# A residual block of attention and a gated MLP: score tiles moved from the attention stage to the projection stage, and one PSUM copy moved to VectorE

## The chip, the cores and the metric

The kernel runs on one core of one Trainium2 chip. The metric is device time in microseconds; of the kernel before, three runs gave 1596.11, 1596.20 and 1596.48 us, the median is 1596.2 us. A core has a matrix engine (TensorE, PE in the profile; its weight loads are listed apart as PEld), a vector engine (VectorE, DVE), a scalar engine (ScalarE, ACT), a general engine (GpSimd, POOL) and a queue engine that starts transfers (SyncE, SP). TensorE writes to PSUM, which here is used as eight tiles ("banks") of 128 x 512 float32.

## What is computed

The input is x, 2048 tokens of 512 features. With 32 heads of 16 features:

```
xn = layernorm(x)
q, k, v = split(xn @ wqkv)                      # 32 heads of 16
p = softmax(q @ k.T / 4)                        # per head, 2048 x 2048
s = (p @ v) @ wo
g = silu(gelu(xn @ w1 + b1) @ w2 + b2)          # 1376 hidden features
out = x + s * g
```

For the softmax the kernel subtracts from every score the maximum of its query's row. The scores are therefore computed twice: once with queries on the partitions, only to find the row maxima, and once transposed, with keys on the partitions, where the (negated) maximum is added through two more contraction rows and the exponential is taken. This document calls the first kind **score tiles** and the second kind **transposed tiles**.

## The kernel before, in words

The work is cut into 32 **units** u: eight groups g of four heads, times four chunks c of 512 queries (`g, c = divmod(u, 4)`). A unit has 64 score tiles (128 queries x 512 keys of one head; two heads run on the two halves, "sides", of TensorE's rows at the same time) and 64 transposed tiles (16 blocks of 128 keys x 4 heads). All 2048 score tiles are made in the order of the list `heads`, unit after unit, well ahead of the transposed tiles of the same unit, because the maxima have to be transposed (`s_end1`, line 265), copied, written to DRAM and loaded back (`load_mh`, line 148) first.

**First stage (projections).** Layer norm, v, q, k and the two MLP products run as float32r pieces of 64 rows, two at a time on the two sides of TensorE (`run` and `mm`, lines 584 to 622; all at L591). Between them `fill` (line 564) puts score tiles, the "early" ones. `LEAD` is their number in units of four: 144, so 576 tiles, nine units. `ROWS` (line 562) is the number of matmuls that one side has left, so a side gets its next early tile once its count `row[a]` has reached `FILL0 + put + made * ROWS / (4 * LEAD)`. A score tile is one matmul (L183) into one of two banks, `ps_a` or `ps_b` (the ring `s_ring`, handed out in turn by `s_tile`, line 92), and one VectorE reduction with max over 512 columns (L189), after which the bank is free again.

**Second stage (attention).** It is a hand-written order of steps n = 0 to 512 (lines 967 to 985). Step n makes the four transposed tiles of unit n // 16 and key block n % 16 (letter T: one matmul at L740, one exponential on ScalarE at L742) and adds the block of the step before to the unit's sum p @ v (letter V: `pv_step`, eight matmuls at L805 into the one bank `ps_v`). The transposed tiles rotate through four banks. The rest of the score tiles is spread over the steps by `due(n)`: two in step 1, three in each of the steps 2 to 491, none later. The strings in `ORDER` (line 40) say how: with three tiles `TXSTTSTYV`, where S is a whole score tile and X and Y are the halves of a third one, one for each side, joined in one bank; with none `TTTTV`. Y waits for a token that passes through GpSimd's queue (lines 221 and 228). The ring of the score tiles has three banks here (`ps_x` joins at line 774).

When a unit's 16th block has been added (V of step 16u + 16), its 128 x 512 sums are copied from PSUM to SBUF by ScalarE (L812), so that `ps_v` is free for the next unit; the last unit's copy is shared by ScalarE and VectorE (L814, L815). One step later SyncE's queue moves the copied rows on (`o_move`), later the denominators are inverted (`o_den`) and multiplied in by GpSimd (`o_div`).

Keys: the buffers `kts` hold three groups (KB = 3). Group 3 takes the place of group 0, whose last reader is unit 3's transposed tiles (steps 48 to 63; step 48 + b reads key block b). Its keys are loaded by six transfers of GpSimd's queue in steps 56 to 61 (first half of the keys) and six in steps 64 to 69. Unit 12, the first of group 3, makes its score tiles in the order of the key chunks of 512 (`at_of`, line 172).

**Tail.** From step 492 on, when no score tiles are left, finished tokens are projected by `wo` (`w_token`, `w_mul`) and gated.

Of the kernel before, what the change touches and what calls it, by code (L numbers as in the profile page):

```python
# [10 lines left out]
AF = mybir.ActivationFunctionType  # L11
# [6 lines left out]
S = 2048  # L18
# [5 lines left out]
CH = 512  # L24
NCH = S // CH
# [4 lines left out]
EPS = 1e-5  # L30
SCALE = DH ** -0.5
VW = DH + 1
LEAD = 144
NW = 10
EARLY = 4
DONE = 492
FILL0 = 30
HB = 4
W2B = 2
ORDER = {0: "TTTTV", 3: "TXSTTSTYV"}  # L40
HC = CH // 2
PAIRED = 28
KB = 3
# [5 lines left out]
def fused(ctx: ExitStack, tc: tile.TileContext, x, wqk, wv, wo, w1, b1, w2, b2, out):  # L49
    nc = tc.nc  # L50
# [37 lines left out]
    NU = NG * NCH  # L88
# [40 lines left out]
    def q_rows(qs, u, sides=range(2)):  # L129
        g, c = divmod(u, NCH)  # L130
        for a in sides:
            for b, src in enumerate((qk_h, qk_l, qk_h)):
                r = 64 * a + DH * b
                nc.sync.dma_start(qs[r:r + DH].bitcast(F32), rows(src, g, 0, a, c * CH, CH))

    def load_qs(u, sides=range(2)):
        if u < NU:
            QS[u] = qzs[u % 2] if u < LEAD // 16 else qss[0][:, u % 2]
            q_rows(QS[u], u, sides)
# [18 lines left out]
    def units_of(u):  # L158
        return (u,) if u >= PAIRED else (u - u % 2, u - u % 2 + 1)

    def tick():
        for e in later:
            e[0] -= 1

    def flush():
        while later and later[0][0] <= 0:
            u = later.pop(0)[1]
            run_off()
            s_end1(u)
            s_end2(u)  # L170
# [38 lines left out]
    def s_op(op):  # L209
        if op == "S":  # L210
            if whole:
                s_whole(whole.pop(), 1)
            else:
                whole.append(jobs.pop(0))
                s_whole(whole[0], 0)
        elif op == "X":
            if not cut:
                cut[:] = [jobs.pop(0), 0]
            ps, pool = s_tile(True)
            x = s_mm(ps, cut[0], 0, 0, cut[1] * HC, HC)  # L220
            token = nc.gpsimd.nop().ins
            tc.add_manual_dep(token, x.name, SYNC, reason="row tile done")
            cut[2:] = [ps, pool, token]
            run_off()
        else:
            job, n, ps, pool, token = cut
            y = s_mm(ps, job, 1, HC, n * HC, HC)
            tc.add_manual_dep(y, token.name, SYNC, reason="other row tile")
            s_max(ps, job, slice(0, 2), n)
            s_ring.append(pool)  # L230
            cut[1] += 1
            if n:
                cut.clear()
# [72 lines left out]
    for i in range(nu):  # L306
        pairs.append(ms[2 * i:2 * i + 2])
        if (i + 1) * len(qs) // nu > i * len(qs) // nu:
            g, c = qs[i * len(qs) // nu]
# [4 lines left out]
    for j in range(len(pairs)):  # L314
        for h in range(2):
# [4 lines left out]
            due = next((i for i in range(j, len(pairs)) if is_m[i]), len(pairs))  # L320
            nxt = next((i for i in range(j + h, len(pairs)) if is_m[i]), len(pairs))
            left = 2 * (nxt - j) + 1 - h
            need = 4 * sum(is_m[:nxt]) - 4 - nd
            room = 2 * (due + 1 - j) - h
            n = 2 if nd < len(parts) and parts[nd][2] and ready - nd > room else 1
            n = max(n, need - 2 * (left - 1))
# [234 lines left out]
    ndown = sum(1 for e in plan if e[0] == "down")  # L561
    ROWS = 12 * (4 * VQ + 2 * len(pairs)) + 6 * ndown - 10 + 2 * LEAD - 2 * (LEAD // 32) - FILL0

    def fill(a):
        due = FILL0 + put[0] + sum(made) * ROWS // (4 * LEAD)
        if sum(made) < 4 * LEAD and row[a] >= due and (made[0] <= made[1]) == (a == 0):
            taken()
            if later and later[0][0] <= 0:
                put[0] += 2
                u = later.pop(0)[1]  # L570
                s_end1(u)
                s_end2(u)
                return
            s_one(a)
            row[a] += 1
            tick()

    def taken():
        prog["pe"] += 1
        s_when.append(prog["pe"])  # L580
        if len(s_when) > 2:
            prog["seen"] = max(prog["seen"], s_when[-3])
# [150 lines left out]
    def t_one(u, k, p, a):  # L733
        g = u // NCH
        if (u, k) not in PT:
            PT[u, k] = slot(3 + len(PN) % 3, (P, GH, CH))
            PN.append(1)
        ps = t_tile()
        r = slice(64 * a, 64 * a + 3 * DH + 2)
        nc.tensor.matmul(ps, kts[g % KB][p][r, k * P:(k + 1) * P],  # L740
                         QT[u][r, p, :], start=True, stop=True)
        nc.scalar.activation(PT[u, k][:, 2 * p + a, :], ps, AF.Exp, scale=SCALE)  # L742
# [55 lines left out]
    PV, OS, DN, DR = {}, {}, {}, {}  # L798
    def pv_step(u, k):
        g = u // NCH  # L800
        if k == 0:
            PV[u] = ps_v.tile([P, CH], F32, name="pv")
        for j in range(GH):
            h = (g * GH + j) * VW
            nc.tensor.matmul(PV[u][32 * j:32 * j + 32, :], vsb[:, k, h:h + 32], PT[u, k][:, j, :],  # L805
                             start=(k == 0), stop=(k == NT - 1))
        del PT[u, k]
        if k == NT - 1:
            OS[u] = wb.tile([P, CH], F32, name="os", bufs=1)
            pv = PV.pop(u)  # L810
            if u < NU - 1:
                nc.scalar.activation(OS[u], pv, AF.Copy)  # L812
            else:
                nc.scalar.activation(OS[u][:, :HC], pv[:, :HC], AF.Copy)  # L814
                nc.vector.tensor_copy(OS[u][:, HC:], pv[:, HC:])  # L815
# [104 lines left out]
    def at(n, f, *a, pos=3):  # L920
        todo.setdefault((n, pos), []).append((f, a))

    KS = tuple(range(KT))
    L = 16 * NU

    def due(n):
        return min(4 * L, 4 * LEAD + max(0, 3 * n - 1))

    for u in range(NU):
        g, c = divmod(u, NCH)  # L930
        if c == 0 and g == KB:
            for i in range(6):
                at(56 + i, load_k, g, (i,), nc.gpsimd, 0, S // 2)
                at(64 + i, load_k, g, (i,), nc.gpsimd, S // 2, S // 2)
        elif c == 0 and g > KB:
            for i in range(6):
                at(64 * (g - KB + 1) + 6 + i, load_k, g, (i,), nc.gpsimd)
        if u >= 2:
            at(16 * u - 14, load_qt, u)
            need = min(n for n in range(L) if due(n) >= 64 * (units_of(u)[-1] + 1)) + (4 if u < NU - 1 else 2)  # L940
            at(max(16 * u - 14, need), load_mh, u)
        if u < NU - 1:
            at(16 * u + 17, o_move, u, pos=0)
            at(16 * u + (25 if u < NU - 2 else 19), o_den, u, pos=0)
            at(16 * u + (31 if u < NU - 2 else 22), o_div, u, nc.gpsimd)
    T3 = range(NT - NCH, NT)
    late = range(NW, NT)
    for t in range(NW):
        n = DONE + 2 * t
# [6 lines left out]
    for i, t in enumerate(late):  # L956
        n = L - 2 * len(late) - 1 + 2 * i
# [8 lines left out]
    jobs.extend(heads[made[0]:])  # L966
    for n in range(L + 1):
        ua, ka = divmod(n, 16)
        want = due(n) - due(n - 1)
        i = 0  # L970
        for op in ORDER[want] if n > 1 else ("TTTTV", "TTSTSVT")[n]:
            if op in "SXY":
                s_op(op)
            elif op == "V":
                if n:
                    pv_step(*divmod(n - 1, 16))
                for _ in range(4):
                    tick()
                flush()
            else:  # L980
                if EARLY <= 4 * n + i < 4 * L:
                    t_one(ua, ka, i % 2, 1 - i // 2)
                for f, args in todo.get((n, i), []):
                    f(*args)
                i += 1
# [54 lines left out]
```

## Time and profile before

| | |
|---|---|
| median of three runs | 1596.2 us |
| span of the profiled execution, first to last instruction | 1594.7 us |
| median less span | 1.5 us |
| granted TensorE clock | 1.000 |
| busy, share of the span: PE / PEld / DVE / ACT / POOL | 100% / 57% / 87% / 79% / 23% |
| score reductions L189 | 2048, mean 685 ns |
| exponentials L742 | 2048, mean 612 and 613 ns |
| first stage with early score tiles | about 59 to 476 us |
| steps with score tiles | about 476 to 1507 us |

The profiled execution's own time is its span; the median of the runs lies 1.5 us above it. Durations are those of single instructions; consecutive instructions of an engine overlap at their ends, so that 2048 exponentials of 612 ns fill less than 2048 times 612 ns, and an engine's busy time counts such an overlap once. The starts of PE's matmuls are recorded, their ends are modelled. A weight load (PEld) belongs to the matmul after it and carries that matmul's wait for a free bank, so it is the instruction to look at when one asks what held a matmul back.

### The profile page before, as it was taken

How to read it: one execution, taken by the hardware profiler on the slowest of the kernel's cores; microseconds unless marked ns; L12 is line 12 of the kernel's file. 1: busy time of each engine (PE TensorE's matmuls, PEld its weight loads, DVE VectorE, ACT ScalarE, POOL GpSimd, SP SyncE). 2: the span in 40 equal slices, each digit the busy share in tenths (PEclk: the TensorE clock that was granted, in tenths of full speed). 3: DMA queues.
4: the chain of work that ended last, by engine and by line, in shares of the span. 5: the costliest groups of instructions: out<-in, count | busy, mean ns of one | idle time of the engine just before them, and what ended most of it. 6: DMA issues, size and time to landing. Idle time of an engine off the chain costs nothing.

```text
span 1594.7 us, 32234 instructions
## 1 busy us (share of the span) xinstructions
PE 1587.6 (100%) x12144; PEld 913.2 (57%) x12144; DVE 1382.8 (87%) x2261; ACT 1260.1 (79%) x2520; POOL 373.0 (23%) x394
## 2 busy tenths in 40 slices
PE   9999999999999999999999999999999999999998
PEld 8899999999884444444444444444444444444445
DVE  7598898989888999999999989999999999999735
ACT  4324333434349999999999999999999999999984
POOL 4145575756650001000100200100010000000142
PEclk9999999999999999999999999999999999999999
DMA  6626343454431113111410411311131111110252
GB/s 205 150 59 164 106 135 107 158 140 123 126 93 54 32 35 66 29 39 44 82 30 21 71 40 30 61 39 29 31 70 30 31 29 36 36 29 22 59 192 100
DMA packets 74651, 116.89 MB, mean 73 GB/s; under 512 B 23012, under 2 KB 24292, under 8 KB 73320
## 3 DMA queue, kind: packets, MB, share of 16 engines
q1 hardware_dynamic: 70748, 101.89, 22.8%
q0 software_dynamic: 3264, 12.35, 3.9%
q8 instruction: 96, 1.57, 0.4%
q14 instruction: 59, 0.48, 0.1%
q10 hardware_dynamic: 484, 0.60, 0.1%
HBM read 84.35 MB, written 25.97 MB: 69 GB/s over the span
## 4 chain that ended last, share of the span: by engine, by line
PE 98%; DVE 1%; DMA 1%; POOL 0%; issue 0%; ACT 0%; SPq 0%; DVEq 0%; POOLq 0%
PE pv L805 32%; PE ps L183 18%; PE pst L740 16%; PE ps L591 12%; PE pst L591 7%; PE ps L740 5%; PE ps L80 3%; PE pv L591 2%; PE ps L459 1%; PE pst L80 1%; DMA raw<-in_wqk 0%; DVE st L418 0%; PE pst L441 0%; DMA xt<-in_x 0%; PE pst L459 0%
## 5 line engine op out<-in xcount | busy, mean ns | idle before, releaser
L189 DVE TENSOR_REDUCE mx<-ps 128x2 f32<-128x512 f32 x2048 | 1299.5, 685 | 149.4 <-PE ps L183 68.8
L742 ACT ACTIVATE slot<-pst 128x512 f32<-128x512 f32 x1533 | 831.0, 612 | 21.6 <-PE pst L740 12.7
L805 PE MATMUL pv<-slot,vsb 128*32 128x512 f32 x4096 | 545.3, 605 | 0.0
L183 PE MATMUL ps<-kt,slot 48*128 48x512 f32 (+1 forms) x1364 | 393.5, 376 | 0.0
L740 PE MATMUL pst<-qt,kt 50*128 50x512 f32 x1149 | 372.7, 432 | 0.6 <-DVE gt L673 0.4
L740 PEld LDWEIGHTS pst<-qt,kt 50*128 50x128 f32 x1149 | 178.6, 184 | 279.9 <-ACT slot L742 264.3
L742 ACT ACTIVATE slot<-ps 128x512 f32<-128x512 f32 x515 | 315.5, 613 | 3.7 <-PE ps L740 0.5
L183 PEld LDWEIGHTS ps<-kt,slot 48*128 48x128 f32 x1364 | 210.6, 184 | 34.8 <-DVE mx L189 21.6
L591 PE MATMUL ps<-slot,w1h 64*128 64x512 f32 x1088 | 218.0, 393 | 0.2 <-ACT junk L605 0.2
L183 PE MATMUL ps<-kt,qz 48*128 48x512 f32 x512 | 212.4, 415 | 0.0
L183 PE MATMUL ps<-slot,slot 48*128 48x512 f32 (+1 forms) x598 | 172.8, 376 | 0.0
L740 PE MATMUL ps<-qt,kt 50*128 50x512 f32 x387 | 160.3, 416 | 0.0
L591 PEld LDWEIGHTS ps<-slot,w1h 64*128 64x128 f32 x1088 | 151.4, 185 | 8.3 <-ACT junk L605 2.7
L805 PEld LDWEIGHTS pv<-slot,vsb 128*32 128x32 f32 x4096 | 80.6, 108 | 120.2 <-issue 112.2
L591 PE MATMUL ps<-slot,w1l 64*128 64x512 f32 x544 | 141.7, 393 | 0.0
L378 POOL TENSOR_TENSOR hl<-hg,hh 128x512 fp32r<-128x512 f32 x76 | 96.7, 1295 | 129.6 <-ACT hh L377 82.5
L605 ACT ACTIVATE junk<-ident_r 1x1 f32<-1x1 f32 x92 | 18.0, 196 | 120.8 <-PE pst L591 113.6
L740 PE MATMUL pst<-qt,slot 50*128 50x512 f32 x384 | 112.5, 415 | 0.0
L251 POOL CAST nmh<-nm 128x16 fp32r<-128x16 f32 x32 | 6.3, 197 | 413.7 <-PE pst L740 184.7
L183 PEld LDWEIGHTS ps<-kt,qz 48*128 48x128 f32 x512 | 93.7, 183 | 16.3
L183 PEld LDWEIGHTS ps<-slot,slot 48*128 48x128 f32 x598 | 92.5, 184 | 15.7 <-DVE mx L189 10.9
L740 PEld LDWEIGHTS ps<-qt,kt 50*128 50x128 f32 x387 | 71.1, 184 | 44.0 <-ACT slot L742 42.8
(159 smaller groups left out, 1699.7 us busy)
## 6 DMA issues: line engine op xcount, KB each, us to landing
raw<-in_w SPq DMA_DIRECT2D x88, 256.0 KB
qk_h<-hh SPq DMA_DIRECT2D x32, 256.0 KB
qk_l<-hl SPq DMA_DIRECT2D x32, 256.0 KB
qt<-qk_h SPq DMA_DIRECT2D x128, 64.0 KB
slot<-qk_h SPq DMA_DIRECT2D x92, 64.0 KB
g_d<-gt POOLq DMA_DIRECT2D x16, 256.0 KB, 3.5
qt<-qk_l SPq DMA_DIRECT2D x64, 64.0 KB
dn<-den_d SPq DMA_DIRECT2D x32, 128.0 KB
```

The costliest lines, as they stand in the source:

```text
L80: nc.tensor.matmul(ps, lhs[a], rhs[b], start=first and n == 0, stop=last and n == 2)
L183: return nc.tensor.matmul(ps[:, c0:c0 + w], QS[u][r, p, qi * P:(qi + 1) * P], kts[u // NCH % KB][p][r, k0:k0 + w], start=True, stop=True).ins
L189: nc.vector.tensor_reduce(MX[u][:, 2 * p:2 * p + 2, qi, ki][:, heads, parts], ps.rearrange("p (n c) -> p n c", c=HC), axis=AX.X, op=OP.max)
L251: nc.gpsimd.tensor_copy(hl[:, 0], nm)
L378: nc.gpsimd.tensor_sub(hl, raw, hh.bitcast(F32))
L459: nc.tensor.matmul(pq["q", g, c], W1[g][i][:, k * P:(k + 1) * P], (xh, xl)[j][c][:, k], start=n == 0 and k == 0, stop=n == 2 and k == KT - 1)
L591: i = nc.tensor.matmul(ps, lhs[r], rhs[r], start=first, stop=last).ins
L605: i = nc.scalar.activation(junk[:, :1], ident_r[:1, :1].bitcast(F32), AF.Copy).ins
L740: nc.tensor.matmul(ps, kts[g % KB][p][r, k * P:(k + 1) * P], QT[u][r, p, :], start=True, stop=True)
L742: nc.scalar.activation(PT[u, k][:, 2 * p + a, :], ps, AF.Exp, scale=SCALE)
L805: nc.tensor.matmul(PV[u][32 * j:32 * j + 32, :], vsb[:, k, h:h + 32], PT[u, k][:, j, :], start=(k == 0), stop=(k == NT - 1))
```

## The change

The number of early score tiles goes from 576 to 608 (nine and a half units). The attention steps get a table `tiles` in place of the formula `due`: step 1 makes two score tiles; from then on a step makes three, but two in the steps 8, 16, 24, 32, 40, 48, 56, 64 and after that in every sixteenth (80, 96, ... 480) and in step 492, where the last two are made. That is 36 steps with two and 456 with three, 1440 tiles. A step with two has the order `TSTTSTV`. The copy of a unit's sums (L812) is done by VectorE; it falls into the steps 16, 32, ... 480, each of which makes two score tiles, and for unit 30 into step 496, which makes none. The fourth group's keys (group 3) are loaded in four quarters of 512 keys, six transfers each, two to a step: quarter q in the steps 51 + 4q to 53 + 4q. The maxima are loaded five steps, not four, after the step in which their last score tile is due (the last unit's still two).

```diff
-LEAD = 144
+LEAD = 152
...
-ORDER = {0: "TTTTV", 3: "TXSTTSTYV"}
+ORDER = {0: "TTTTV", 2: "TSTTSTV", 3: "TXSTTSTYV"}
...
             if u < NU - 1:
-                nc.scalar.activation(OS[u], pv, AF.Copy)
+                nc.vector.tensor_copy(OS[u], pv)
...
-    def due(n):
-        return min(4 * L, 4 * LEAD + max(0, 3 * n - 1))
+    tiles = [0, 2]
+    while 4 * LEAD + sum(tiles) < 4 * L:
+        left = 4 * (L - LEAD) - sum(tiles)
+        tiles.append(2 if len(tiles) % (8 if len(tiles) < 60 else 16) == 0 or left in (2, 4) else 3)
+    tiles += [0] * (L + 1 - len(tiles))
+    assert sum(tiles) == 4 * (L - LEAD) and tiles.count(3) % 2 == 0
+    due = [4 * LEAD + sum(tiles[:n + 1]) for n in range(L + 1)]
...
         if c == 0 and g == KB:
-            for i in range(6):
-                at(56 + i, load_k, g, (i,), nc.gpsimd, 0, S // 2)
-                at(64 + i, load_k, g, (i,), nc.gpsimd, S // 2, S // 2)
+            for q in range(NCH):
+                for i in range(6):
+                    at(51 + 4 * q + i // 2, load_k, g, (i,), nc.gpsimd, q * CH, CH)
...
-            need = min(n for n in range(L) if due(n) >= 64 * (units_of(u)[-1] + 1)) + (4 if u < NU - 1 else 2)
+            need = min(n for n in range(L) if due[n] >= 64 * (units_of(u)[-1] + 1)) + (5 if u < NU - 1 else 2)
...
-        want = due(n) - due(n - 1)
         i = 0
-        for op in ORDER[want] if n > 1 else ("TTTTV", "TTSTSVT")[n]:
+        for op in ORDER[tiles[n]] if n > 1 else ("TTTTV", "TTSTSVT")[n]:
```

## The prediction, made before the changed kernel ran

> **What bounds the kernel now.** I read the table by stretches first, then each stage by its own waits.
>
> ```profile
> core 0 of [0], span 1594.7 us
> core 0: us, PE busy (x) PEld busy (x) DVE busy (x) ACT busy (x) POOL busy (x), PEclk, DMA share, GB/s
> 280.00:320.00 40.00, 40.00 (x338) 36.24 (x337) 36.07 (x58) 17.73 (x41) 31.63 (x30) 1.00 0.47 151
> 1040.00:1080.00 40.00, 40.00 (x311) 17.22 (x312) 36.43 (x61) 39.23 (x79) 2.98 (x4) 1.00 0.13 32
> 1520.00:1560.00 40.00, 40.00 (x226) 18.37 (x220) 15.54 (x19) 34.01 (x67) 18.77 (x15) 1.00 0.61 204
> ```
> After a stretch stands its length, then busy times. PE looks full everywhere, so that column decides nothing. The first stage (row 1) has ACT at 18 of 40 us and DVE at 36. The attention steps (row 2) have DVE at 36 and ACT at 39. The change takes work from the second kind and adds to the first, so the question is what one more tile costs in the first and what one less, and a copy less on ACT, is worth in the second.
>
> **First stage.** Here stand two of VectorE's reductions, the next but one of each other, then weight loads of score matmuls, each with start and duration:
>
> ```profile
> 300.54 0.68 DVE L189 TENSOR_REDUCE mx<-ps 128x2 f32<-128x512 f32 x1
> 301.94 0.68 DVE L189 TENSOR_REDUCE mx<-ps 128x2 f32<-128x512 f32 x1
> ```
> ```profile
> 301.27 0.18 PEld L183 LDWEIGHTS ps<-kt,qz 48*128 48x128 f32 x1
> 302.68 0.18 PEld L183 LDWEIGHTS ps<-kt,qz 48*128 48x128 f32 x1
> ```
> These reductions end at 301.22 and 302.62; score weight loads start at 301.27 and 302.68, about 0.05 us later. With two banks a score tile waits for the reduction two before it. The round of one bank is: weight load at 301.27, reduction of that tile from 301.94 to 302.62, next weight load at 302.68. That is 1.41 us, in which two tiles are made, one in each bank. TensorE alone would be a little quicker: before the first early tile it ran
>
> ```profile
> 54.85 2.75 PE pst L591 x24
> ```
> 0.1146 us a matmul, so the twelve matmuls between a bank's two uses take 1.375 us. The two limits are 3% apart, and what happens with fewer matmuls in between is seen where the order happens to bring the tiles closer:
>
> ```profile
> 320.95 0.39 PE L183 MATMUL ps<-kt,qz 48*128 48x512 f32 x1
> 321.16 0.39 PE L591 MATMUL ps<-slot,w1h 64*128 64x512 f32 x1
> 321.18 0.39 PE L591 MATMUL ps<-slot,w1l 64*128 64x512 f32 x1
> 321.40 0.44 PE L183 MATMUL ps<-kt,qz 48*128 48x512 f32 x1
> 321.41 0.67 PE L591 MATMUL ps<-slot,w1h 64*128 64x512 f32 x3
> 321.88 0.43 PE L591 MATMUL ps<-slot,w1l 64*128 64x512 f32 x2
> 322.11 0.43 PE L591 MATMUL ps<-slot,w1h 64*128 64x512 f32 x2
> 322.34 0.39 PE L183 MATMUL ps<-kt,qz 48*128 48x512 f32 x1
> ```
> From the first L183 to the third there are 11 matmuls, 1.26 us of TensorE, and it took 1.39. A shorter gap isn't passed quicker: about 1.39 us for two tiles, 0.695 each, is the floor of the two-bank round. Over the whole stage a tile takes more, with the interruptions in it:
>
> ```profile
> L189 DVE TENSOR_REDUCE mx<-ps x542: 678/690/694, 80.1 to 469.6; 128x2 f32<-128x512 f32 x181
> ```
> 541 intervals in 389.5 us, 0.720 us each.
>
> **Attention steps.** V's matmuls mark the steps (start, duration); ScalarE's rows stand below:
>
> ```profile
> 1014.92 1.06 PE L805 MATMUL pv<-slot,vsb 128*32 128x512 f32 x8
> ...
> 1017.30 1.06 PE L805 MATMUL pv<-slot,vsb 128*32 128x512 f32 x8
> ...
> 1019.32 1.07 PE L805 MATMUL pv<-slot,vsb 128*32 128x512 f32 x8
> ...
> 1021.43 1.06 PE L805 MATMUL pv<-slot,vsb 128*32 128x512 f32 x8
> ```
> ```profile
> 1013.29 0.60 ACT L742 ACTIVATE slot<-ps 128x512 f32<-128x512 f32 x1
> 1013.76 0.62 ACT L742 ACTIVATE slot<-pst 128x512 f32<-128x512 f32 x1
> 1014.24 0.63 ACT L812 ACTIVATE os<-pv 128x512 f32<-128x512 f32 x1
> 1014.72 0.64 ACT L742 ACTIVATE slot<-pst 128x512 f32<-128x512 f32 x1
> ```
> Ordinary steps alternate, here 2.02 and 2.11 us, 2.07 on average. The step that comes after the copy takes 2.38, 0.31 more: the copy holds ScalarE from 1014.24 to 1014.72, 0.48 us, the exponentials behind it come late, and the transposed tiles wait for their banks. A whole unit agrees (chain of work):
>
> ```profile
> 1252.22 1.06 PE pv L805 x8
> 1285.58 1.06 PE pv L805 x8
> ```
> 33.36 us, 16 x 2.07 and 0.24 over.
>
> **The change, part by part.**
>
> *32 more early tiles.* The side's matmul count, ROWS, is 1728 now, exactly 3.0 a tile, and becomes 1744 for 608, 2.868 a tile (the MLP's matmuls stay the same). So one side's next tile comes after six rows in 74% of cases and after five in 26%; in all matmuls, twelve or about ten between a bank's uses. Six-row tiles go on at 0.720. Five-row tiles go at the floor, 0.695, as the 11-matmul stretch did. The mean is 0.7135: 608 x 0.7135 = 433.8 us against 576 x 0.720 = 414.7, **+19.1 us**. Bounds: all at 0.720 gives +23.0; all at the floor, 422.6, gives +7.9. The bound below these would be a TensorE slot a tile, 32 x 0.1146 = +3.7, which the 1.39 us for 11 matmuls speaks against; it is a rival. In the row of 280 to 320 us weight loads are busy 36.24 of 40 us. The Trainium skill's page "Perfetto Trace Analysis", section "Identifying the Most-Contended Engine", says that TensorE's headroom is judged by its weight-load share and not by its matmul share; at 90% that makes TensorE the limit here, and an added tile would cost its slot, the rival's +3.7 in place of +19.1. The weight loads that start 0.05 us after a reduction's end speak for the banks.
>
> *The copy off ScalarE.* It ends 30 units within the steps that have score tiles (16 to 480); the 31st copy, in step 496, lies in the tail, where DVE is busy 15.54 of 40 us. What goes is 0.31 us a unit. What is late next: V of the next unit now waits for VectorE. The nearest rows for that copy are half of it and a reduction of the same size:
>
> ```profile
> L815 DVE COPY os<-pv x1: 424/424/424, 1574.1 to 1574.1; 128x256 f32<-128x256 f32 x1
> ```
> so 0.42 to 0.85 us; I take 0.69, that of the reduction, which also reads 512 columns. A V lasts 1.07 us and the next starts about 2.0 after it, so the copy has 0.9 us: neither 0.69 nor 0.85 makes that V wait. Queued behind it on VectorE are the next step's reductions, and for those wait the score matmuls' banks. The copy stands where the third reduction stood, so I put their delay at 0.
>
> *Two tiles, not three, in these steps.* TensorE has one tile less, 0.11 us; VectorE's work stays (a copy for a reduction) and ScalarE's four exponentials stay. Those two set 2.07 as much as PE does, so I take 0.05 of the 0.11. Gain a unit 0.36, **-10.8 us** in 30 units; bounds 0 (the copy costs VectorE's chain what ScalarE's gained) and 0.42 x 30 = 12.6. The four further two-tile steps (8, 24, 40, 56): -0.2, between 0 and -0.4.
>
> *One step more with tiles.* Step 492 is already a projecting one; two tiles add two matmuls and two reductions: +0.4, between +0.2 and +1.4. The last maxima are sent a step later, with two tail steps left; a tail step is V to V
>
> ```profile
> 1509.82 1.06 PE L805 MATMUL pv<-slot,vsb 128*32 128x512 f32 x8
> ...
> 1513.24 1.06 PE L805 MATMUL pv<-slot,vsb 128*32 128x512 f32 x8
> ```
> 3.4 us, so this should hide.
>
> *Keys in quarters.* 24 GpSimd transfers for 12, two a step:
>
> ```profile
> L109 POOL DMA_DIRECT2D kt<-qk_h x20: 497/514/559, 593.8 to 1168.1; - x20
> ...
> DMA to landing us min/median/max: 2.9/5.0/7.0
> ```
> Two issues take 1.03 us of GpSimd in a step of 2.07, behind the step's X token and ahead of the next. The first quarter's last issue is in step 53, its tiles start in step 57; three steps between are 6.2 us. Cost 0, cover: GpSimd's idle time (3 of 40 us busy); with a landing of 7.0 it would be about 1 us once. Group 4 keeps five free steps. The later load of the maxima is one step in many: 0.
>
> **Sum** on the profiled execution: 1594.7 + 19.1 - 10.8 - 0.2 + 0.4 = 1603.2; the median lies 1.5 above the span: **1604.7 us**.
>
> **Rivals.**
> *A, TensorE's slots set the first stage* (+3.7 in place of +19.1): 1589.3 us, faster. For it: PE is busy 40.00 of 40 us. It decides if the round of a bank can shrink below 1.39 us when matmuls are fewer; the 11-matmul stretch is against it.
> *B, VectorE's chain takes back the gain*: the copy can't start before V ends, the reductions behind it come late, and score matmuls wait for banks. Gain 0: 1604.7 + 10.8 = 1615.5. For it: DVE 36.43 of 40 busy; against: a reduction leaves for the copy.
> *C, both stages are milder*: first stage at the floor (+7.9) with the gain kept: 1593.5, no change by my bound.
> *D, the freed ScalarE shortens every step* to the quicker 2.03: 0.04 x 490 = 20 us less, 1585. Against: VectorE's wait remains.
>
> **Chances.** Forecast 0.66, A 0.14, B 0.10, C 0.06, D 0.04. The forecast's own range, first stage +14 to +23, steps -7 to -12.6, is 1597.5 to 1612. To hold eight in ten it goes down to A and C: 1589 to 1612; B and D are out. A measurement tells 0.2%, 3.2 us, from no change: faster A and D, 0.18; same C and the forecast's low edge, 0.10; slower 0.72.
>
> **What would show it.** First stage: reductions still at about 0.71 us a tile and the first exponentials some 19 us later (A: 4 us); weight loads still 0.05 us after reductions. Steps: no 2.38 us step, units without maxima near 33.0; V never waiting for the copy. I am wrong if the tiles of the first stage come nearer than 0.69 us, or if a step behind the copy stays long.

## The result and the profile after

The changed kernel takes 1609.56 us, the median of four runs (1609.14 to 1609.81), against 1596.15 (1595.99 to 1596.48) for the kernel before on the same chip: a ratio of 1.0084, 95% interval 1.0072 to 1.0097. It is slower by 13.4 us. The profiled execution has a span of 1608.0 us against 1594.7, with a granted clock of 1.000 in both.

To split the 13.3 us I cut both traces at two instructions that they share: the first weight load of a transposed tile (step 0 begins) and that of step 496 (the tail begins). All stage times below are made in this way.

| stage | before | after | difference | predicted |
|---|---|---|---|---|
| start to step 0 | 473.95 | 495.45 | +21.5 | +19.1 |
| steps 0 to 496 | 1046.80 | 1038.56 | -8.2 | -10.6 |
| step 496 to the end | 73.93 | 74.02 | +0.1 | 0 |

The beginning of the attention stage can be read directly off ScalarE's first exponentials, here of the kernel before and then of the changed one (start, duration):

```profile
475.01 2.48 ACT L742 ACTIVATE slot<-ps 128x512 f32<-128x512 f32 x5
```
```profile
496.50 2.48 ACT L742 ACTIVATE slot<-ps 128x512 f32<-128x512 f32 x5
```

They come 21.5 us later. The rows of the first stage and of the attention steps in the table by stretches of the changed kernel, with the columns that they had before:

```profile
280.00:320.00 40.00, 40.00 (x327) 35.26 (x324) 36.35 (x58) 17.53 (x39) 27.79 (x25) 1.00 0.42 120
1040.00:1080.00 40.00, 40.00 (x308) 17.49 (x306) 36.66 (x61) 39.06 (x77) 4.77 (x9) 1.00 0.42 68
```

In the first row TensorE is "busy" for 40.00 us again, but it finished 327 matmuls where it had finished 338. VectorE finished the same 58 instructions. The engine whose busy time says 100% became slower, and the pace of the other did not change. The early tiles' reductions, over the whole stage of the changed kernel:

```profile
L189 DVE TENSOR_REDUCE mx<-ps x544: 678/690/693, 80.1 to 469.7; 128x2 f32<-128x512 f32 x182
```

543 intervals in 389.6 us are 0.7175 us each, where there were 0.720. Over all 608 early tiles the mean is 0.7172, and 608 x 0.7172 - 576 x 0.7200 = 21.3 us: the whole delay of the first stage is the extra tiles at an almost unchanged pace.

Groups of weight loads from 80 to 470 us, the same score tiles in each; behind the second bar is the idle time ahead of them. First the kernel before, then the changed one:

```profile
L183 PEld LDWEIGHTS ps<-kt,qz 48*128 48x128 f32 x482 | 88.2, 183 | 15.3
```
```profile
L183 PEld LDWEIGHTS ps<-kt,qz 48*128 48x128 f32 x482 | 88.2, 183 | 23.0 <-DVE mx L189 7.0
```

As many loads of the same length, with 23.0 us of waiting ahead of them in place of 15.3; the first releaser that the profile now names is the reduction.

A place where the tiles stand densely shows how the wait works. TensorE of the changed kernel, and below it VectorE:

```profile
286.71 0.44 PE L183 MATMUL ps<-kt,qz 48*128 48x512 f32 x1
286.86 0.53 PE L591 MATMUL ps<-slot,w1h 64*128 64x512 f32 x2
287.09 0.53 PE L591 MATMUL ps<-slot,w1l 64*128 64x512 f32 x2
287.32 0.53 PE L591 MATMUL ps<-slot,w1h 64*128 64x512 f32 x2
287.56 0.40 PE L183 MATMUL ps<-kt,qz 48*128 48x512 f32 x1
287.69 0.49 PE L591 MATMUL ps<-slot,w1h 64*128 64x512 f32 x2
288.05 0.50 PE L183 MATMUL ps<-kt,qz 48*128 48x512 f32 x1
...
289.54 0.45 PE L183 MATMUL ps<-kt,qz 48*128 48x512 f32 x1
```
```profile
285.92 2.08 DVE L189 TENSOR_REDUCE mx<-ps 128x2 f32<-128x512 f32 x3
288.15 1.29 DVE L189 TENSOR_REDUCE mx<-ps 128x2 f32<-128x512 f32 x2 [0.16 <-PE ps L591]
```

The tiles alternate between two banks, so the tile at 288.05 needs the bank of the one at 286.71. Its reduction is the last of three that end at 288.00 (285.92 + 2.08), and the tile starts 0.05 later. At the stage's 0.115 us a matmul, TensorE could have gone on after the two from 287.69 at 287.92, and it stood still for 0.13. From 286.71 to 288.05 are ten matmuls in 1.34 us; the next use of that bank comes at 289.54, twelve matmuls and 1.49 us later. In the whole stage 585 of 606 score weight loads start 0.050 to 0.055 us after the end of the reduction two tiles before, which freed their bank (before 553 of 574).

In the attention steps the copy is now among VectorE's work. One unit's end, by V's matmuls and by VectorE:

```profile
1030.14 1.07 PE L805 MATMUL pv<-slot,vsb 128*32 128x512 f32 x8
1032.16 1.06 PE L805 MATMUL pv<-slot,vsb 128*32 128x512 f32 x8
1034.35 1.06 PE L805 MATMUL pv<-slot,vsb 128*32 128x512 f32 x8
1036.37 1.06 PE L805 MATMUL pv<-slot,vsb 128*32 128x512 f32 x8
```
```profile
1031.27 0.69 DVE L812 COPY os<-pv 128x512 f32<-128x512 f32 x1 [0.35 <-PE pv L805]
1031.88 3.81 DVE L189 TENSOR_REDUCE mx<-ps 128x2 f32<-128x512 f32 x6
```

The unit's last V starts at 1030.14. The steps by V's starts are 2.02, **2.19** and 2.02 us. The step of 2.38 is gone, and a step of 2.19 is left in its place; over the 30 units it lasts from 2.00 to 2.28 us, 2.16 on average, where before it lasted 2.37 to 2.39. VectorE stands still for 0.35 us until V ends, copies for 0.69, and then has six reductions without a pause: it is behind with the score tiles, and one of these waits. The score weight load in the long step:

```profile
1033.81 0.18 PEld L183 LDWEIGHTS ps<-slot,slot 48*128 48x128 f32 x1 [0.25 <-DVE mx L189]
```

It stood still for 0.25 us until a reduction freed its bank, and the step is 0.17 longer than the next.

### The profile page after: what moved, and what is told of

Same layout as the page of the kernel before. It is cut to its first block, busy times and chain, and to the rows that moved or that the text cites. A ratio compares the mean times of both kernels' runs of the same rounds, so it can differ in the third digit from the quotient of the medians.

```text
span 1608.0 us, 32141 instructions
## 1 busy us (share of the span) xinstructions
PE 1601.6 (100%) x12110; PEld 921.6 (57%) x12110; DVE 1402.9 (87%) x2292; ACT 1249.0 (78%) x2489; POOL 378.6 (24%) x406
## 4 chain that ended last, share of the span: by engine, by line
PE 99%; DVE 1%; issue 0%; ACT 0%; POOL 0%; DVEq 0%; POOLq 0%
PE pv L805 32%; PE ps L183 19%; PE pst L740 16%; PE ps L591 13%; PE pst L591 7%; PE ps L740 5%; PE ps L80 3%; PE pv L591 2%; PE ps L459 1%; PE pst L80 1%; PE pv L492 1%; PE pst L441 0%; PE pst L459 0%; DVE slot L75 0%; PE ps L441 0%; DVE st L418 0%
## 5 line engine op out<-in xcount | busy, mean ns | idle before, releaser
L742 ACT ACTIVATE slot<-ps 128x512 f32<-128x512 f32 x515 | 310.7, 604 | 3.7 <-PE ps L740 1.1
L591 PE MATMUL ps<-slot,w1h 64*128 64x512 f32 x1088 | 228.1, 394 | 0.0
L183 PE MATMUL ps<-kt,qz 48*128 48x512 f32 x512 | 223.3, 437 | 0.0
L591 PEld LDWEIGHTS ps<-slot,w1h 64*128 64x128 f32 x1088 | 155.5, 185 | 8.0 <-ACT junk L605 1.8
L591 PE MATMUL ps<-slot,w1l 64*128 64x512 f32 x544 | 148.2, 393 | 0.0
L740 PE MATMUL pst<-qt,slot 50*128 50x512 f32 x384 | 106.8, 411 | 0.0
L371 ACT ACTIVATE hg<-ps,b_sb 128x512 f32<-128x512 f32 x44 | 27.9, 685 | 78.9 <-PE ps L591 71.9
```

Source lines behind the costliest of these rows:

```text
L183: return nc.tensor.matmul(ps[:, c0:c0 + w], QS[u][r, p, qi * P:(qi + 1) * P], kts[u // NCH % KB][p][r, k0:k0 + w], start=True, stop=True).ins
L371: nc.scalar.activation(raw, ph.pop(u), AF.Gelu_apprx_tanh, bias=b1_sb[:, u[2]:u[2] + 1])
L591: i = nc.tensor.matmul(ps, lhs[r], rhs[r], start=first, stop=last).ins
L740: nc.tensor.matmul(ps, kts[g % KB][p][r, k * P:(k + 1) * P], QT[u][r, p, :], start=True, stop=True)
```

## The experiments

Two disputes were to be settled. In the first stage: **my theory**, the round of the two banks (matmul, VectorE's reduction, next weight load) sets the pace of the early tiles; **rival A**, a tile costs its slot on TensorE. In the steps: **my theory**, the copy on VectorE and the missing third tile together take the long step away; **rivals**, one of the two does it alone, or VectorE's chain takes the gain back (B). Every ratio is to the kernel before on the same chip, with its 95% interval.

| kernel | median us | ratio | step 0 starts | steps 0 to 496 |
|---|---|---|---|---|
| before | 1596.2 | | 473.95 | 1046.80 |
| changed | 1609.56 | 1.0084 [1.0072, 1.0097] | 495.45 | 1038.56 |
| half_before | 1590.03 | 0.9959 [0.9943, 0.9975] | 467.48 | 1046.95 |
| half_after | 1585.23 | 0.9929 [0.9907, 0.9950] | 470.45 | 1038.85 |
| late_start | 1621.75 | 1.0158 [1.0143, 1.0173] | 499.04 | 1046.92 |
| fill20 | 1595.70 | 0.9999 [0.9990, 1.0008] | 473.32 | 1046.59 |
| act_copy | 1618.69 | 1.0139 [1.0124, 1.0154] | 495.71 | 1046.71 |
| dve_copy | 1596.84 | 1.0004 [0.9994, 1.0013] | 473.36 | 1047.44 |
| split_copy | 1602.34 | 1.0037 [1.0023, 1.0051] | 473.40 | 1053.16 |
| early_only | 1622.12 | 1.0159 [1.0141, 1.0177] | 495.20 | 1051.68 |
| shifted | 1611.69 | 1.0098 [1.0083, 1.0114] | 495.18 | 1040.19 |
| keys_quarters | 1596.38 | 1.0002 [0.9993, 1.0011] | 473.85 | 1046.55 |

### The first stage: reductions of half the length

The kernel before and the changed kernel, each with early reductions that read half of the columns, so that a bank comes free sooner (the row maxima of the early tiles leave out the other half):

```diff
+        cols = ps.rearrange("p (n c) -> p n c", c=HC)
+        if "seen" in prog:
+            cols = cols[:, :, :HC // 2]
-        nc.vector.tensor_reduce(MX[u][:, 2 * p:2 * p + 2, qi, ki][:, heads, parts], ps.rearrange("p (n c) -> p n c", c=HC), axis=AX.X, op=OP.max)
+        nc.vector.tensor_reduce(MX[u][:, 2 * p:2 * p + 2, qi, ki][:, heads, parts], cols, axis=AX.X, op=OP.max)
...
-        nc.scalar.activation(PT[u, k][:, 2 * p + a, :], ps, AF.Exp, scale=SCALE)
+        nc.scalar.activation(PT[u, k][:, 2 * p + a, :], ps, AF.Exp, scale=SCALE / 64)
```

> The kernel before, in which the reduction of an early tile reads half of its columns (the row maxima of these tiles leave out the other half, and the exponentials are scaled down by 64). The reduction falls from 0.69 us to about 0.42 us, so VectorE and the two banks are no limit any more. Theory: the first stage runs at TensorE's pace, its first exponential comes at 460 to 465 us in place of 475. Rival A (TensorE's slots are the limit already): no change, 474 to 476 us.

> The changed kernel with the same half reductions of the early tiles. Theory: without the limit of VectorE and the banks the 32 added tiles cost TensorE's slots only, so the first exponential comes 3 to 6 us later than with half reductions in the kernel before, not 21.5 us as between the whole kernels. Rival (the tiles are dear for another reason, their order among the matmuls, or waits of the two sides for each other): again some 20 us later.

Early reductions of the two kernels, 90 to 460 us (half_before, then half_after):

```profile
L192 DVE TENSOR_REDUCE mx<-ps x522: 424/425/428, 89.7 to 459.9; 128x2 f32<-128x256 f32 x174
```
```profile
L192 DVE TENSOR_REDUCE mx<-ps x546: 414/425/427, 90.3 to 459.5; 128x2 f32<-128x256 f32 x182
```

and where the first exponentials stand (in the same order):

```profile
468.64 2.48 ACT L745 ACTIVATE slot<-ps 128x512 f32<-128x512 f32 x5
```
```profile
471.61 2.48 ACT L745 ACTIVATE slot<-ps 128x512 f32<-128x512 f32 x5
```

A reduction now takes 0.425 us, not 0.690, and in the same 370 us there are 546 of them against 522: the tiles do come closer, 0.677 us against 0.709, which they did not with the long reduction (0.7172 against 0.7200). The tiles now follow the rows: 0.709 / 3.0 and 0.677 / 2.868 are both 0.236 us a row, TensorE's pace, where with the long reduction the time of a *tile* is constant. The 32 additional tiles delay step 0 by 470.45 - 467.48 = 2.97 us in place of 21.5, at the lower edge of the expected 3 to 6. That is 0.093 us a tile, close to TensorE's slot of 0.1146: with the banks' round out of the way, rival A's price holds. Nothing but the length of the reductions (and a constant in the exponential, whose duration did not change) differs between the two pairs, so the round through VectorE is shown to be what 18.5 of the 21.5 us were lost to. These two kernels shorten VectorE's own work together with the round. That the round through two banks is the limit, and not VectorE alone, is read from the traces: the loads start 0.05 us after the release, and in the attention steps, with three banks, VectorE gets through six reductions in 3.81 us (shown above), by my estimate 0.62 from one start to the next, less than the 0.717 of the first stage. No run gave the first stage a third bank. The change then wins: 1585.0 to 1585.5 us against 1589.8 to 1590.4, because its gain in the steps (1046.95 - 1038.85 = 8.1 us) is all that is left to see.

half_before alone was a miss in size: its first exponentials were expected at 460 to 465 us and came at 468.64, 6.4 us sooner than before. At a tile in three rows, TensorE's own pace is only that far off the banks'.

### The first stage: the same tiles, more densely or less

`FILL0` is the row at which the early tiles begin. With 150 for 30 the 576 tiles are left with fewer rows each, without one tile more; with 20 they have a little more room.

```diff
-FILL0 = 30
+FILL0 = 150      # late_start
+FILL0 = 20       # fill20
```

> The kernel before with FILL0 = 150 for 30: the same 576 early tiles and the same matmuls, but the first stage runs 120 more rows a side without tiles, and then a side gets its next tile after 2.79 rows on average in place of 3.0. Theory (the round through two banks and VectorE sets the pace of the tiles, about 0.72 us each however few matmuls stand between): the tile-free part adds up to 27 us and little of it comes back, 1609 to 1623 us, tiles still 0.69 to 0.72 us apart. Rival A of the prediction (a tile costs TensorE's slot): the same work in another order, 1596 to 1599 us, tiles 0.67 us apart.

> The kernel before with FILL0 = 20 for 30: the first early tile comes ten rows a side, 2.3 us, earlier. Theory (the early tiles' pace through VectorE and two banks sets the first stage, so their start counts): the whole 2.3 us is gained, 1593.5 to 1595 us. Rival (the first tile would wait for its keys, which are still on their way): 1596 us or more.

First exponentials of late_start, then the reductions of late_start and of fill20 between 90 and 460 us:

```profile
500.12 2.48 ACT L742 ACTIVATE slot<-ps 128x512 f32<-128x512 f32 x5
```
```profile
L189 DVE TENSOR_REDUCE mx<-ps x519: 679/690/694, 89.5 to 459.9; 128x2 f32<-128x512 f32 x173
```
```profile
L189 DVE TENSOR_REDUCE mx<-ps x512: 678/690/694, 89.8 to 459.6; 128x2 f32<-128x512 f32 x171
```

Late_start came within its range, 1609 to 1623 us. It adds no work, and step 0 comes 25.1 us later. TensorE's slots would have made that nothing: the same matmuls, only in another order. But the stage's tiles need about 0.716 us each, with fewer rows between them too, and beginning later only moves the end. Put together, rows per tile (1728 less `FILL0` - 30, or 1744, by the tiles) and mean pitch over all early tiles were 2.79 and 0.7159 us (late_start), 2.868 and 0.7172 (changed), 3.0 and 0.7200 (before), 3.017 and 0.7226 (fill20). The pitch is nearly flat up to 3.0 and is higher at 3.017. So the order before stands near a corner, at which TensorE and the banks cost almost the same: 0.709 us a tile by TensorE's pace in half_before, 0.716 by the banks in late_start. fill20 was expected to bring its whole earlier start, 2.3 us (its first reduction at 56.9 in place of 59.2), and that failed: there is no difference in the medians. Its step 0 comes 0.6 us sooner than in the kernel before, but it does so in dve_copy and split_copy too (table above), whose first stage is that of the kernel before. The earlier start is used up by the longer pitch; why the pitch rises there isn't shown, since 3.017 rows at 0.236 us are only 0.712.

### The steps: copy and tile count, one without the other

act_copy is the changed kernel with the copy back on ScalarE; dve_copy is the kernel before with the copy on VectorE and still three tiles in every step.

```diff
-                nc.vector.tensor_copy(OS[u], pv)
+                nc.scalar.activation(OS[u], pv, AF.Copy)     # act_copy, to the changed kernel
...
-                nc.scalar.activation(OS[u], pv, AF.Copy)
+                nc.vector.tensor_copy(OS[u], pv)             # dve_copy, to the kernel before
```

> The changed kernel with the copy of a unit's sums back on ScalarE; the 608 early tiles and the two-tile steps stay. Theory (the steps' gain comes from the copy leaving ScalarE, the two-tile step is only its room): the copy holds ScalarE 0.48 us again, a unit is 0.2 to 0.3 us longer than in the changed kernel, the time is 1616 to 1619 us, and the first stage stays as in the changed kernel (first exponential at 496.5 us). Rival (the missing tile gave the gain, wherever the copy runs): within 2 us of 1609.6.

> The kernel before with one edit: the copy of a unit's sums on VectorE, in steps that still make three score tiles. Theory (VectorE is as full as ScalarE in a three-tile step, so the copy needs the room of a tile): four operations at about 0.6 us do not fit into 2.07 us, the steps at a unit's end are at least as long as with ScalarE's copy, 1596 to 1606 us. Rival (ScalarE alone is the limit there): all of 0.31 us a unit is gained, about 1587 us.

Four kernels fill a table of two by two; steps 0 to 496 take

| | three tiles at a unit's end | two tiles |
|---|---|---|
| copy on ScalarE | 1046.80 | 1046.71 |
| copy on VectorE | 1047.44 | **1038.56** |

The kernels on the right also make 32 score tiles fewer in the steps and load keys and maxima as in the change. Neither part alone is worth anything; only both together are. act_copy and dve_copy came within the ranges of their theories, and both rivals failed. V's starts about a unit's end in act_copy, then in dve_copy:

```profile
1036.74 1.07 PE L805 MATMUL pv<-slot,vsb 128*32 128x512 f32 x8
1039.12 1.06 PE L805 MATMUL pv<-slot,vsb 128*32 128x512 f32 x8
```
```profile
1012.61 1.06 PE L805 MATMUL pv<-slot,vsb 128*32 128x512 f32 x8
1014.71 1.06 PE L805 MATMUL pv<-slot,vsb 128*32 128x512 f32 x8
1017.05 1.06 PE L805 MATMUL pv<-slot,vsb 128*32 128x512 f32 x8
```

Both still have the long step, 2.38 and 2.34 us, for different reasons. In act_copy ScalarE still holds the copy, and the tile that was taken out of the step was not what the step waited for. In dve_copy ScalarE is free, but VectorE has the copy on top of three reductions:

```profile
1012.17 1.89 DVE L189 TENSOR_REDUCE mx<-ps 128x2 f32<-128x512 f32 x3 [0.16 <-PE ps L183]
1013.98 0.68 DVE L812 COPY os<-pv 128x512 f32<-128x512 f32 x1
1014.57 2.56 DVE L189 TENSOR_REDUCE mx<-ps 128x2 f32<-128x512 f32 x4
```

From 1012.17 to 1017.13 it doesn't pause. The copy can start only when the unit's last V has ended (1013.67) and waits here for the third reduction until 1013.98; the reductions behind it are 0.6 us late, and the banks of the score tiles with them. That is rival B's mechanism, in a kernel in which no reduction leaves for the copy.

### The steps: a copy in two halves

To the kernel before, with three tiles; each engine copies half of the columns.

```diff
-                nc.scalar.activation(OS[u], pv, AF.Copy)
+                nc.scalar.activation(OS[u][:, :HC], pv[:, :HC], AF.Copy)
+                nc.vector.tensor_copy(OS[u][:, HC:], pv[:, HC:])
```

> The kernel before with one edit: half of the copied columns by ScalarE and half by VectorE, in steps that still make three score tiles. Theory (each engine has some 0.1 to 0.2 us of slack before a delay shows): each delay is smaller than the present 0.31 us and they overlap, 1589 to 1595 us. Rival (two engines are disturbed where one was): 1596 to 1602 us.

My own expectation failed, and with 1602.3 us the time lies just above the rival's range too. The steps take 6.4 us more than before. V's starts, then ScalarE's half and VectorE's half:

```profile
1015.55 1.07 PE L805 MATMUL pv<-slot,vsb 128*32 128x512 f32 x8
1017.82 1.06 PE L805 MATMUL pv<-slot,vsb 128*32 128x512 f32 x8 [0.17 <-DVE os L813]
1020.16 1.06 PE L805 MATMUL pv<-slot,vsb 128*32 128x512 f32 x8
```
```profile
1016.89 0.41 ACT L812 ACTIVATE os<-pv 128x256 f32<-128x256 f32 x1
```
```profile
1017.34 0.42 DVE L813 COPY os<-pv 128x256 f32<-128x256 f32 x1 [0.36 <-ACT os L812]
```

The two steps after the copy last 2.27 and 2.34 us. The two halves did not run side by side: VectorE's starts 0.03 us after ScalarE's has ended, in all 31 units, with VectorE idle for 0.36 us ahead of it here. The next V starts 0.05 us after VectorE's half, so it waits for both in a row; in the step after that the work behind both halves is late. The overlap that the expectation counted on didn't take place. Why the second half waits for the first isn't shown, and so this run doesn't tell what two halves at the same time would cost.

### The steps: where the missing tile stands

early_only has the copy on ScalarE and two-tile steps only up to step 56 and at the very end, so that the tiles which the change takes out at the units' ends come off the end of the score tiles (after step 483 there are none). shifted has the copy on VectorE and two tiles in the step *after* the copy's (17, 33, ...), where the copy's successors are.

```diff
-        tiles.append(2 if len(tiles) % (8 if len(tiles) < 60 else 16) == 0 or left in (2, 4) else 3)
+        tiles.append(2 if len(tiles) < 60 and len(tiles) % 8 == 0 or left in (2, 4) else 3)      # early_only
+        tiles.append(2 if len(tiles) > 8 and len(tiles) % (8 if len(tiles) < 60 else 16) == 1 or left in (2, 4) else 3)      # shifted
```

> The changed kernel with ScalarE's copy, and with two-tile steps only up to step 56 and at the end: the 32 tiles fewer leave the last steps, and score tiles end some eight steps earlier. Theory (a step of transposed tiles alone is still held by ScalarE's four exponentials, about 1.9 us): only some 0.1 to 0.2 us is saved in each of these steps, so the time is about that of the kernel with ScalarE's copy and two-tile steps, 1616 to 1620 us. Rival (a tile less is worth its third of a step, 0.69 us, here): 1600 to 1606 us.

> The changed kernel with its two-tile steps one step later (9, 17, 25, ... 57, 65, 81, ... 481): the copy on VectorE now comes out of a step with three tiles, and the step behind it makes two. Theory (VectorE reaches the copy only when V has ended, so the copy burdens the step behind, where now a reduction is missing, but it also comes later, behind the third reduction, and the next unit's V waits for it): what is left behind the copy, 0.13 us in the third step, goes, and some 0.1 to 0.2 us of waiting comes; steps 0 to 496 within 3 us of the changed kernel's 1038.6, total 1607 to 1613 us. Rival (only the room in the copy's own step counts): no gain over the kernel before's steps, 1046 to 1048 us, total 1617 to 1619 us.

early_only came at 1622.1 for an expected 1616 to 1620. Its trace has a pause that the changed kernel does not have, in the steps 142 to 144:

```profile
792.70 1.07 PE L805 MATMUL pv<-slot,vsb 128*32 128x512 f32 x8
798.21 1.93 PE L805 MATMUL pv<-slot,vsb 128*32 128x512 f32 x8
...
804.51 1.06 PE L805 MATMUL pv<-slot,vsb 128*32 128x512 f32 x8
```

Three steps in 11.81 us, 5.6 over the usual 6.2. The score tiles of unit 16 come a step earlier in this kernel than in the changed one. The last transfer of their keys is issued at 788.66 and lands 8.6 us later, at 797.22; the first score weight load behind the pause starts at 797.28, after TensorE has stood still for 2.77 us. That is what tiles waiting for their keys would look like; no run moved the transfer by itself. The rest of the loss comes behind the pause: the granted clock is 0.50 from 796.4 to 803.2 us, and V's eight matmuls take 1.93 us in place of 1.07.

```profile
799.00:801.00 2.00, 2.00 (x13) 0.93 (x7) 0.40 (x1) 0.09 (x1) 0.00 (x0) 0.50 0.44 98
```

Without the pause the steps would take 1046, as before. The tiles taken off the end bought nothing, and the table by stretches shows why, in 16 us of steps without any score tile:

```profile
1516.00:1532.00 16.00, 16.00 (x97) 5.48 (x89) 1.21 (x4) 15.68 (x33) 0.42 (x2) 1.00 0.42 130
```

VectorE has 1.21 us of work, ScalarE 15.68 of 16. Five of these steps, by V's starts:

```profile
1521.95 1.06 PE L805 MATMUL pv<-slot,vsb 128*32 128x512 f32 x8
...
1532.06 1.07 PE L805 MATMUL pv<-slot,vsb 128*32 128x512 f32 x8
```

10.11 us, 2.02 each: ScalarE sets them. A step with three tiles, 2.08 us on average away from the units' ends in act_copy, is hardly longer than one with none. Here, taking a tile away shortened a step only where something else had to fit into its time.

shifted came within its range and gained 6.6 of the 8.2 us. VectorE at a unit's end, and V's next start:

```profile
1028.25 3.91 DVE L189 TENSOR_REDUCE mx<-ps 128x2 f32<-128x512 f32 x6 [0.35 <-PE ps L183]
1032.07 0.68 DVE L812 COPY os<-pv 128x512 f32<-128x512 f32 x1
```
```profile
1030.73 1.06 PE L805 MATMUL pv<-slot,vsb 128*32 128x512 f32 x8
1032.81 1.06 PE L805 MATMUL pv<-slot,vsb 128*32 128x512 f32 x8
```

The unit's last V ends at 1031.79, but the copy stands behind six reductions until 1032.07; it ends at 1032.75, and the next V starts at 1032.81. Here V itself waits for the copy.

The mean steps around the copy, in the order copy's step, the next, the one after, over 30 units are 2.064, 2.160 and 2.019 here and 2.016, 2.074 and 2.156 in the changed kernel (2.062, 2.079, 2.382 before). Where the missing tile makes room, the lateness goes from one step to its neighbour; it doesn't vanish.

### The keys alone

The kernel before with the fourth group's keys in quarters, as in the change.

```diff
-            for i in range(6):
-                at(56 + i, load_k, g, (i,), nc.gpsimd, 0, S // 2)
-                at(64 + i, load_k, g, (i,), nc.gpsimd, S // 2, S // 2)
+            for q in range(NCH):
+                for i in range(6):
+                    at(51 + 4 * q + i // 2, load_k, g, (i,), nc.gpsimd, q * CH, CH)
```

> The kernel before with one edit: the fourth group's keys in quarters from step 51 on. Theory (24 issues are hidden in GpSimd's idle time): 1595.5 to 1596.9 us. Rival (two issues a step hold back the tokens that pass through GpSimd's queue): 1597 to 1600 us, with longer steps from 51 to 66.

1596.38 us, ratio 1.0002 [0.9993, 1.0011]; steps 1046.55. That is within the theory's range: no effect that can be measured.

No version with all of the computation beat the kernel before.

## Why the prediction was right, point by point

The forecast was 1604.7 us and the time 1609.56; the side and the mechanism of both stages came out as argued, and the 4.9 us between come from two terms that were mis-sized in the same direction. One piece of the evidence was misread, though.

- **The bank round sets the first stage: right, and shown.** Shorter reductions took 18.5 of the 21.5 us away; denser tiles without more of them cost 25 us; weight loads stand 0.05 us behind reductions. Rival A's price appears as soon as the round is shortened. The rule of the Trainium skill, page "Perfetto Trace Analysis", section "Identifying the Most-Contended Engine", judges TensorE's headroom by its weight-load share (and by MFU, the share of the peak rate that its matmuls reach). The weight loads were busy 36.24 of 40 us before, but VectorE was busy 36.07, so the shares don't tell the two apart. The runs agree that TensorE was near its pace (half_before came only 6.4 us sooner), but the price of one more tile was 0.67 us by the measured 21.5 / 32, not a TensorE slot; the measurement decides.
- **The 11-matmul stretch was no evidence against A.** The prediction took its 1.39 us for the floor of the two-bank round. With half reductions the same three tiles of the kernel before (from 316.77 to 318.18 us in half_before) take 1.41 us, although their banks are free almost 0.3 us before their weight loads start, and all pairs of tiles with eleven matmuls from one to the other have a median of 1.39 us there. So 1.39 us is TensorE's own pace in that order, as rival A would have it, and that 0.695 us lies near the pace of the banks is luck. What did speak for the banks were the weight loads 0.05 us behind the reductions.
- **The size, +19.1, was 2.4 us short.** The step that failed is "five-row tiles go at the floor, 0.695", together with "six-row tiles go on at 0.720". Pairs with ten matmuls went more quickly than that, 1.335 us on average in 111 cases (0.668 a tile, nearer than the 0.69 that the prediction gave as a sign of being wrong; with half reductions such pairs take 1.167). But pairs with twelve went more slowly, 1.446 in place of the 1.421 of the kernel before (the 0.720 of the forecast, 1.44 a pair, held the stage's interruptions too). The mean, 0.717, hardly moved. The round is a rate, not a floor of the single gap: a tile that starts early after its bank comes free leaves the next one behind the same reductions. My bound "all at 0.720", +23.0, was nearer than my middle.
- **The copy and the third tile: -10.8 forecast, -8.2 measured.** The term that was mis-sized is "I put their delay at 0" for the reductions behind the copy. The second step behind the unit's last V has 2.156 us on average, not 2.07, where it had 2.382, so 0.226 and not 0.31 went there; the copy's own step gave 0.046, the 0.05 that I took. Together that is 0.27, by 30 units 8.2. The sign "a step behind the copy stays long" thus came true in small part. The argument "the copy stands where the third reduction stood" overlooked that a reduction can start as soon as its tile is made, and the copy only when V has ended: VectorE's idle 0.35 us ahead of it, which the trace shows, is where I put the loss; no run took that idle time away by itself.
- **V doesn't wait for the copy: right, though the profile's list seems to say otherwise.** The lines of the copy in the changed kernel:

```profile
L812 DVE COPY os<-pv x31: 681/692/693, 532.5 to 1537.8; 128x512 f32<-128x512 f32 x31
...
  PEld pv L805: 6.2, 28
```

  By this list V's weight load waited for the copy at 28 units, 6.2 us in all. But the list puts an idle time down to whatever semaphore came last in it, and in the unit shown above the copy ends at 1031.96 and V starts 0.20 later; over the 30 units it is 0.14 to 0.67. What really waits starts about 0.05 us after its release, as the first stage's weight loads do, and as V does behind the copy in the kernel before (0.05 to 0.07 in all 30), in dve_copy and nearly always in act_copy and shifted. See also the last score matmul ahead of V, in the step with the copy and in the next:

```profile
1031.93 0.28 PE L183 MATMUL ps<-slot,slot 48*128 48x256 f32 x1
...
1034.15 0.27 PE L183 MATMUL ps<-slot,slot 48*128 48x256 f32 x1
```

  V follows 0.23 us later (1032.16) in the first and 0.20 later (1034.35) in the second, where there is no copy: most of that idle time is there anyway. The duration, 0.692 us, is the 0.69 that I took.
- **What could be told apart only afterwards.** I had the gain of a unit as the sum of two terms, 0.31 for the copy and 0.05 for the tile. The two-by-two table shows that they aren't terms of a sum: each is worth nothing alone. Rival B was the state of affairs without the missing tile.
- **Keys in quarters, later maxima, step 492: 0 or nearly, not contradicted.** The keys were tried alone; the other two weren't, and the sums leave little room for them.
- **Rivals C and D:** the tiles as a whole didn't go at the floor, and the steps away from the units' ends stayed as they were, 2.083 us on average and 2.085 before.

## What to carry to other kernels

Before work is moved into a stage in which every engine looks busy, find the round that sets its pace (buffer, producer, consumer, release) and price the added work by that round: less other work between two uses of a buffer may not quicken it. An operation moved to another engine needs a hole there of its own length at the moment when its input is ready, and making the hole and moving the operation have to be tried together, since each alone can be worth nothing. Before a listed wait is believed, compare the time from release to start with that of a wait that is certain. When an engine is said to be 100% busy, count its finished instructions per stretch of time: a modelled end hides the waits.

## What was unexpected of the hardware

- TensorE's busy column stayed at 40.00 of 40 us with 344 matmuls in the stretch (half_after), 338 (before) and 327 (changed), at a granted clock of 1.00 in all three:

```profile
280.00:320.00 40.00, 40.00 (x344) 34.14 (x343) 25.33 (x61) 15.97 (x36) 31.72 (x30) 1.00 0.50 146
```

  This is half_after, whose VectorE needs 25.33 us for more tiles; the count of matmuls, not the busy time, shows the wait that went.
- VectorE's copy of a whole bank, 128 x 512 float32, takes 0.692 us and the reduction over it 0.690; half of the columns take 0.425. By these two lengths 256 columns of a reduction cost 0.265 us, and an estimated 0.16 of each doesn't depend on the length.
